# One Trainium2 core, a long convolution followed by a maxout FFN: the two sums over k1 of a tile placed step by step, and the first loop's stores, turns and drain rearranged

## The chip, the cores and the metric

The kernel runs on one core of a Trainium2 chip. The metric is device time in microseconds (us), the median of several executions. The profile is one execution, recorded instruction by instruction.

## The reference

Two layers follow each other. The first is a convolution as long as the sequence, computed with FFTs, whose filter comes from a small MLP; its output is multiplied by `x`. The second is a feed-forward layer that takes the maximum of three projections.

```python
# x, v: (4, 12544, 128); pos_emb: (12544, 64)
h_filt = (np.maximum(pos_emb @ w1, 0.0) @ w2) * np.exp(-0.01 * np.arange(S))[:, None]
u = x * v
Uf = np.fft.rfft(u, n=2 * S, axis=1)
Hf = np.fft.rfft(h_filt, n=2 * S, axis=0)
y = np.fft.irfft(Uf * Hf[None, :, :], n=2 * S, axis=1)[:, :S, :]
x = (x * y).reshape(B * S, 128)
h = np.maximum(np.maximum(x @ moe_w1, x @ moe_w2), x @ moe_w3)    # (50176, 768)
out = h @ moe_w_out                                               # (50176, 128)
```

All of it is float32.

## The kernel before, in words

TensorE (PE) does the transforms as matrix products in two stages, one over blocks of the sequence (index `k1`, 90 values, taken as 45 pairs `g`) and one inside a block. Besides PE there are VectorE (DVE), ScalarE (ACT), GpSimd (POOL) and the queue engine SyncE (SP). Every engine works through its own instructions in the order in which the Python code issues them[...]. A tile of a pool with `bufs=n` can be given out again only when the readers of the n-th tile before it are done, DMAs included. [...] a product that needs a bank waits until the engine that copies the former one out is done.

**Before the first loop** the filter and the first batch are brought into the first stage's spectrum.

**The first loop** (lines 991 to 1025) has one step `s` per pair `g`, 45 and a few to run out. PE does in a step, in this order: `s_second(s)` (`gps`, filter), `g_second(s)` (`ps`, signal), `s_filter(s-1)` (`sps`, two banks, one such tile), `g_third(s-3)` (`ps` again, from the pool `cps` of three banks that `g_second` uses too). Around them:

- `s_minus` (L931): POOL makes `minus`, the negated part of `specH`, for the next step's `gps`; one buffer.
- ACT copies `G` out of `gps`, `eo` out of `ps`, makes the two halves of `xs` (L547, L548), copies `ht` out of `sps` (L966) and `zs` out of the third product (L577).
- `ht` (two buffers) is multiplied in by DVE in `g_re` and `g_im`, and stored to `hd` in DRAM by two DMAs that POOL issues (L969), directly behind the copy. Later batches read `hd`.
- `zs` (two buffers) is stored to `zd` in DRAM by a DMA that ACT issues (L578).
- DVE does `g_re`, `g_im`, `g_unfold` (`ab`, which the third product reads) of pair `s-2`, and `g_butterfly` (`xt`) of pair `s`.
- SP loads the weights `wt` of both products three steps ahead (`load_dir`, L843), two loads of 256 KB a step.
- In the last 16 steps the first six units `u` of the second batch are loaded (`u_load`, L358), multiplied (`u_mul`, L365) and turned (`u_turn`: four PE transposes into a bank `pst` of `cps`, then an ACT copy). The turns come in pairs, 0 and 1 in step 36, 2 and 3 in step 41.

**The drain** (lines 988 to 1030) finishes the last pairs, and puts in between what the FFN needs: the product `lin` of `w1` and `w_out`, in six folds (`fold`: a transpose into `pt`, an ACT copy `w1t`, two products into the bank `pl`), and the first stage of six units (`unit`, two `u_first` each: PE products into a bank, ACT copy `high`, two DVE operations into `spec`).

**The FFN** has 32 tiles for each of the four batches. A tile has six steps `f`. In a step, `up` makes two products into the `hps` banks (three, in turn): ACT takes the first through Relu (L710), DVE takes the maximum with the second (L713, `hid`), and `down` of two steps before accumulates into `ops`. While the tiles of batch `b` go through, the convolution of batch `b+1` is spread over the 192 steps by `conv_steps`, a planner that holds an estimated DVE load of each step: `u_...` first, then pairs, each with two `g_quarter` products, `g_fold` (DVE takes the sum and the difference from PSUM, L496, after an ACT copy `eo`), `q_swap`, `q_re`, `q_im` and two `q_unfold`. Functions planned for a step run at its end.

The next tile's input is made beside: `t_load` fetches `zt`, `t_sums` makes the two sums over `k1` (`even` and, in place, `zt`; L678, L679, in half of the tiles L682 on DVE), and `t_last` does the last product and multiplies with `x` into `gt` (L700). Where no pairs are planned the sums run on POOL, else on DVE. Both come at once, in step 0 ahead of `up`:

```python
            if f == (3 if turn_ else 0):
                t_sums(tiles[n + 1], nc.vector if turn_ or i * NF > pairs_from else nc.gpsimd)
```

The planner allows for them with a fixed load in step 0 and for `t_last` with one in step 3:

```python
        load = [(1.2 if i % NF == 3 else 0.6) + (1.4 if i % NF == 0 and i > s0 else 0)
                for i in range(NT * NF)]
```

The last batch has no convolution beside it and another scheme of products; the change doesn't touch it.

Of the kernel before, what the change touches and what calls it, by code (L numbers as in the profile page):

```python
# [10 lines left out]
FP32 = mybir.dt.float32  # L11
# [5 lines left out]
P = 128  # L17
# [8 lines left out]
N1 = 90  # L26
# [65 lines left out]
def kernel(  # L92
# [279 lines left out]
    def u_turn(u):  # L372
        if u % 2 == 0:
            uts[u] = uts[u + 1] = utp.tile([NB, 16, 2, 32], FP32, tag="uT", name="uT")
        ps = state["turn"].tile([P, 512], FP32, tag="cv", name="pst")
        turn(u, ps)
        nc.scalar.copy(uts[u][:, 8 * (u % 2):8 * (u % 2) + 8],
                       ps[0:NB, :].rearrange("n (s t r) -> n s r t", s=8, r=2))
# [190 lines left out]
    def g_third(g):  # L569
        w, ab = ws.pop((g, 1)), abs_.pop(g)  # L570
        ps = state["cv"][1].tile([P, 512], FP32, tag="cv", name="ps3")
        for k in range(2):
            for q in range(2):
                halves_mm(ps[:, (2 * k + q) * D:(2 * k + q + 1) * D], w[:, k, q, :],
                          ab[:, k, q, :], k == 0 and q == 0, True)
        zs = state["cv"][0].tile([P, 2, 256], FP32, tag="z", name="zs", bufs=2)
        nc.scalar.copy(zs[:].rearrange("p k f -> p (k f)"), ps[:])  # L577
        nc.scalar.dma_start(  # L578
            zd[0][2 * g:2 * g + 2].rearrange("k c t f -> (c t) k f"), zs[:])

    def conv_steps(b, done):


        out = []

        def at(slot, late, fn, *args):
            out.append((slot, late, len(out), fn, args))

        per_pair = 170 / (NK + LATE + 0.6 * (NU - done))
        for u in range(done, NU):
            s = (u - done) * 0.6 * per_pair + 9
            at(max(0, int(s) - 9), 0, u_load, b, u)
            at(int(s) - 6, 0, u_mul, u)
            at(int(s) - 5, 0, u_planes, u)
            at(int(s) - 4, 0, u_dma, u)
            at(int(s), 0, u_join, u)
            at(int(s + 1), 1, u_first, u)
        s0 = int((NU - done - 1) * 0.6 * per_pair + 9) + 6  # L600

        def start(x):
            return s0 + int(x // 2 * 2 * per_pair)

        load = [(1.2 if i % NF == 3 else 0.6) + (1.4 if i % NF == 0 and i > s0 else 0)
                for i in range(NT * NF)]
        for x in range(NK + LATE):
            s = start(x)
            load[s] -= 1.2
            load[s + 1 + x % 2] += 1.4  # L610

        def emptiest(among, cost):
            s = min(among, key=lambda i: load[i])
            load[s] += cost
            return s

        for x in range(NK + LATE):
            s, odd = start(x), x % 2
            g, z = x if x < NK else None, x - LATE if x >= LATE else None
            at(s, 1, g_quarter, g, z)  # L620
            at(s + 1 + odd, 0, g_fold, g, z)
            at(s - 4, 0, w_load, x)
            if z is not None:
                at(s + 3 + odd, 0, g_store, b, z)
            if g is None:
                continue
            if g % 2 == 0:
                at(s - 4, 0, q_load, g, min(2, NK - g))
                at(s - 1, 0, h_load, g, min(2, NK - g))
            first = s + 2 + 2 * odd  # L630
            at(first, 0, q_swap, g, 0)
            at(first + 1, 0, q_swap, g, 64)
            last = start(x + LATE) - 1
            a = emptiest(range(first + 1, min(first + 3, last - 1) + 1), 0.7)
            at(a, 0, q_re, g)
            a = emptiest(range(a, min(first + 4, last - 1) + 1), 0.7)
            at(a, 0, q_im, g)
            for q in range(2):
                at(emptiest(range(a + 1, last + 1), 0.55), 0, q_unfold, g, q)
        slots = {}  # L640
        for s, _, _, fn, args in sorted(out, key=lambda r: r[:3]):
            slots.setdefault(s, []).append((fn, args))
        return slots, {start(x) + 1 for x in range(NK + LATE)}, s0


    N = 4 * NB
# [24 lines left out]
                              x[:, 4 * i:4 * i + 8, c, b, :])  # L671
        xTs[b, i], xTs[b, i + 1] = xT[:, 0], xT[:, 1]

    def t_sums(i, eng=nc.gpsimd):
        z0, z1 = zts[i]
        even = hp.tile([N1, 512], FP32, tag="even", name="even", bufs=2)
        if i[0] == 0 or i[1] < NT // 2:
            eng.tensor_tensor(out=even[:], in0=z0, in1=z1, op=ALU.add)  # L678
            eng.tensor_tensor(out=z1, in0=z0, in1=z1, op=ALU.subtract)  # L679
        else:  # L680
            for out, op in ((even[:], ALU.add), (z1, ALU.subtract)):
                nc.vector.scalar_tensor_tensor(out=out, in0=z1, scalar=sign_t[:, 0:1], in1=z0,  # L682
                                               op0=ALU.mult, op1=op)
        zts[i] = even[:], z1

    def t_last(i):
        zt = zts.pop(i)
# [218 lines left out]
    for i in (1, 2):  # L906
# [6 lines left out]
    cps = pro.enter_context(tc.tile_pool(name="cps0", bufs=3, space=PSUM))  # L913
    gps = pro.enter_context(tc.tile_pool(name="gps", bufs=2, space=PSUM))
    sps = pro.enter_context(tc.tile_pool(name="sps", bufs=1, space=PSUM))
    state = {"cv": (cvp, cps), "turn": cps, "xb": 2,
             "bank": lambda: cps.tile([P, 512], FP32, tag="cv", name="ps1")}
    pl = sps.tile([D, 512], FP32, name="pl")
    Gs, minus = {}, {}

    def fold(f):
        pt = cps.tile([P, 512], FP32, tag="cv", name="pt")
        nc.tensor.transpose(pt[:, 0:D], w_sb[0][:, f * P:(f + 1) * P], eye[:])
        w1t = cvp.tile([P, 2, D], FP32, tag="eo", name="w1t", bufs=2)
        nc.scalar.copy(w1t[:, 0], pt[:, 0:D])
        return lambda: halves_mm(pl[:, 0:D], w1t[:, 0], wo_sb[:, f, :], f == 0, f == NF - 1)

# [23 lines left out]
    def s_filter(g):  # L951
# [4 lines left out]
        for ri in range(2):  # L956
            for k in range(2):
                for q in range(2):
                    for h in range(2):
# [5 lines left out]
        ht = cvp.tile([P, 2, 2, 2, D], FP32, tag="ht", name="ht", bufs=2)  # L965
        nc.scalar.copy(ht[:].rearrange("p r k q d -> p (r k) q d"),  # L966
                       ps[:].rearrange("p (q m d) -> p m q d", q=2, d=D))
        for c in range(2):
            nc.gpsimd.dma_start(hd[g, 64 * c:64 * c + 64],  # L969
                                ht[64 * c:64 * c + 64, c].rearrange("p k q d -> p (k q d)"))  # L970
        hts[g] = ht

    EARLY = 6
    loads = dict(zip((NK - 16, NK - 14, NK - 12, NK - 9, NK - 8, NK - 4), range(EARLY)))
    muls = dict(zip((NK - 13, NK - 11, NK - 10, NK - 5, NK - 3, NK - 1), range(EARLY)))
    turns = {NK - 9: 0, NK - 4: 2}
    folded = []

    def folding(f):
# [4 lines left out]
    def unit(u):  # L984
        for h in range(2):
            u_first(u, 2 * h, 2)

    drain = {NK: [lambda: folding(0), lambda: folding(1), lambda: folded.pop()()],
             NK + 1: [lambda: folding(2), lambda: folding(3), lambda: folded.pop()(),
                      lambda: unit(0), lambda: unit(1)]}  # L990
    s_minus(0)
    for s in range(NK + 3):
        if s < NK:
            ws[s, 0] = wf[s]
            s_second(s)
            if s + 1 < NK:
                s_minus(s + 1)
            g_second(s)
            wf.pop(s)
            if s + 3 < NK:  # L1000
                wf[s + 3] = load_dir(s + 3, 0)
        if 1 <= s <= NK:
            g_swap(s - 1)
            s_filter(s - 1)
        if s >= 3:
            ws[s - 3, 1] = wi.pop(s - 3)
            g_third(s - 3)
            if s < NK:
                wi[s] = load_dir(s, 1)
        if 2 <= s <= NK + 1:  # L1010
            g_re(s - 2)
            g_im(s - 2)
            g_unfold(s - 2)
        if s < NK:
            g_butterfly(s)

        if s in muls:
            u_mul(muls[s])
        if s in turns:
            u_turn(turns[s])  # L1020
            u_turn(turns[s] + 1)
        if s in loads:
            u_load(1, loads[s])
        for job in drain.get(s, ()):
            job()
    u_turn(4)
    u_turn(5)
    folding(4)
    folding(5)
    folded.pop()()  # L1030
    nc.scalar.copy(lin[:], pl[:, 0:D])
    for u in range(2, 6):
        unit(u)
    pro.close()


# [22 lines left out]
    late = []  # L1059
    for n, (b, i) in enumerate(tiles[:LAST]):  # L1060
        if i == 0:
            beside, folds, pairs_from = conv_steps(b + 1, EARLY if b == 0 else 0)
        if n == 0:
            t_load(*tiles[0])
            t_load(*tiles[1])
# [2 lines left out]
        for f in range(NF):  # L1068
# [4 lines left out]
            elif i == NT - 1 and f < 2 and n + 1 + f < len(tiles):  # L1073
                t_load(*tiles[n + 1 + f])
            turn_ = i == NT - 1
            if f == 0:
                when = 4 if turn_ else min((3, 4, 2), key=lambda k: i * NF + k in folds)
            if f == (3 if turn_ else 0):
                t_sums(tiles[n + 1], nc.vector if turn_ or i * NF > pairs_from else nc.gpsimd)
            if f == 4 and n + 1 == LAST:  # L1080
                t_sums(tiles[n + 2], nc.vector)
            h = up((b, i), f)
            late.append(((b, i), f, h))
            if len(late) > 2:
                down(*late.pop(0))
            if f == when:
                t_last(tiles[n + 1])
            if f == 5 and n + 1 == LAST:
                t_last(tiles[n + 2])
# [100 lines left out]
```

## Time and profile before

| | |
|---|---|
| time, median of 3 runs | 2310.24 us (2307.21 to 2312.99) |
| profiled execution | 2310.21 us, span of the core 2308.4 us, PE clock 0.997 |
| up to the first loop | 0 to 117.8 us |
| first loop | 117.8 to 298.3 us |
| drain and first tile's input | 298.3 to 323.9 us, PE busy 17.57 of 25.60 us |
| FFN with convolution beside it, three batches | 323.9 to about 1890 us |
| last batch | about 1890 to 2308.4 us |
| DMA, whole run | 411.02 MB, mean 178 GB/s |
| DMA, 200 to 250 us (first loop) | 280 GB/s, mean busy share of the 16 engines 0.94 |

In the lines of the profile, `gps<-wt,minus` means that the instruction writes `gps` and reads `wt` and `minus`. Lines of the timeline have the start and the duration in us, the engine, the line of the code, the operation, the tiles, the shapes and how many were merged; in brackets stands the time for which the engine had been idle before, and who released it. "ACTq" and "SPq" are an engine's queue side, which issues DMAs. PEld is PE's load of weights. The page's shares are averages over stages with different limits.

### The profile page before, as it was taken

What the parts mean: (1) busy time and instruction counts of PE and PEld (TensorE: products, weight loads), DVE (VectorE), ACT (ScalarE), POOL (GpSimd) and SP (SyncE); (2) the same over time, 40 slices, a digit from 0 to 9 for tenths busy, and PEclk for the clock granted to TensorE, in tenths of its full rate; (3) what the DMA queues carried; (4) which work ended last, traced back from release to release, by engine and by line L of the source; (5) the groups of instructions that cost most, each with busy time, mean ns of one, the idle gap of its engine ahead of it and who ended that gap; (6) DMA issues with size and microseconds to landing.
All of it is one profiled execution on the core that took longest, in us unless ns stands there. A gap on an engine that the chain in (4) does not pass through costs nothing.

```text
span 2308.4 us, 68374 instructions
## 1 busy us (share of the span) xinstructions
PE 2270.3 (98%) x27855; PEld 1369.0 (59%) x27855; DVE 1575.3 (68%) x2856; ACT 1179.9 (51%) x2128; POOL 899.7 (39%) x1095
## 2 busy tenths in 40 slices
PE   8999989999999999999999999999999999999998
PEld 7989866655555546655555446655555446666665
DVE  5578856767887847758887847658888854445443
ACT  2678844456666534446666624446666632222222
POOL 2045424423333324423333324423333326666666
PEclk9999999999999999999999999999999999999999
DMA  7778969989998759969999849969999932222221
GB/s 176 191 216 266 289 164 190 157 188 241 234 239 221 197 125 192 187 145 240 247 245 247 211 118 194 186 146 244 246 248 240 221 93 55 55 59 68 65 55 22
DMA packets 473164, 411.02 MB, mean 178 GB/s; under 512 B 328005, under 2 KB 374232, under 8 KB 472850
## 3 DMA queue, kind: packets, MB, share of 16 engines
q1 hardware_dynamic: 433714, 317.68, 62.7%
q0 software_dynamic: 26416, 75.80, 11.3%
q10 hardware_dynamic: 12720, 13.18, 1.8%
q8 instruction: 219, 3.59, 0.7%
q14 instruction: 95, 0.78, 0.1%
HBM read 262.84 MB, written 84.67 MB: 151 GB/s over the span
## 4 chain that ended last, share of the span: by engine, by line
PE 83%; DMA 7%; ACT 3%; DVE 3%; issue 2%; SPq 1%; ACTq 0%; POOL 0%; DVEq 0%; POOLq 0%
PE hps L156 40%; PE ops L156 17%; PE ops L773 6%; PE cps L417 5%; PE cps L156 4%; PE ps L165 3%; PE cps L471 3%; PE cps L481 2%; DMA wt<-wq_const 2%; DMA ht<-hd 2%; DMA hd<-ht 2%; PE last L156 1%; ACT ht L966 1%; PE pst L370 1%; DMA zt<-zd 1%
## 5 line engine op out<-in xcount | busy, mean ns | idle before, releaser
L156 PE MATMUL hps<-gt,w_sb 128*64 128x392 f32 x6144 | 1149.6, 495 | 5.8 <-DVE hid L713 5.0
L710 ACT ACTIVATE hid<-hps 128x392 f32<-128x392 f32 x768 | 384.3, 500 | 734.7 <-PE hps L156 718.8
L156 PEld LDWEIGHTS hps<-gt,w_sb 128*64 128x64 f32 x6144 | 422.4, 137 | 438.7 <-issue 390.1
L713 DVE TENSOR_TENSOR hid<-hid,hps 128x392 f32<-128x392 f32 x768 | 427.8, 557 | 334.0 <-PE hps L156 329.6
L156 PE MATMUL ops<-hid,wo_sb 128*64 128x392 f32 x2304 | 477.9, 492 | 0.0
L523 POOL TENSOR_TENSOR cb<-cb,xs 128x512 f32<-128x512 f32 x135 | 181.9, 1347 | 471.7 <-DVE xs L520 327.1
L156 PEld LDWEIGHTS ops<-hid,wo_sb 128*64 128x64 f32 x2304 | 167.7, 137 | 211.5 <-issue 211.5
L496 DVE TENSOR_TENSOR cb<-cps,eo 128x512 f32<-128x512 f32 (+1 forms) x288 | 175.2, 650 | 66.4 <-ACT eo L493 65.9
L428 DVE TENSOR_TENSOR spec<-cps,high 128x360 f32<-128x360 f32 x180 | 135.2, 792 | 122.8 <-ACT high L426 122.8
L728 POOL DMA_DIRECT2D out_dram<-ot x96 | 75.1, 783 | 353.5 <-ACT ot L726 311.5
L511 ACT ACTIVATE xs<-cb 32x512 f32<-32x512 f32 x270 | 170.0, 630 | 22.6 <-DVE cb L496 13.9
L512 ACT COPY xs<-cb 32x512 f32<-32x512 f32 x270 | 166.7, 617 | 3.2
L426 ACT COPY high<-cps 128x360 f32<-128x360 f32 x90 | 71.9, 799 | 152.4 <-PE cps L417 125.7
L527 DVE TENSOR_TENSOR xs<-cb 128x256 f32<-128x256 f32 x270 | 142.0, 569 | 7.5 <-POOL cb L523 7.5
L417 PEld LDWEIGHTS cps<-f1q,uT 98*64 98x64 f32 x2880 | 124.1, 137 | 31.3 <-issue 30.6
L417 PE MATMUL cps<-f1q,uT 98*64 98x90 f32 x2880 | 127.7, 241 | 0.4 <-DVE uT L401 0.4
L386 POOL COPY planes<-ut 128x784 uint16<-128x784 uint16 x90 | 75.8, 842 | 113.0 <-DVE ut L365 110.2
L504 POOL DMA_DIRECT2D zd<-cb x135 | 92.9, 690 | 61.5 <-DVE cb L496 53.5
L156 PEld LDWEIGHTS cps<-f4p,even 90*64 90x64 f32 x1568 | 88.8, 138 | 37.6 <-issue 34.8
L515 DVE TENSOR_TENSOR cb<-cb,ht 128x512 f32<-128x512 f32 x135 | 92.3, 683 | 7.8 <-ACT xs L512 7.7
L156 PE MATMUL cps<-f4p,even 90*64 90x49 f32 x1568 | 95.7, 220 | 1.8 <-DVE even L678 1.8
L156 PE MATMUL cps<-f4p,zt 90*64 90x49 f32 x1568 | 97.0, 222 | 0.4 <-DVE zt L679 0.4
(137 smaller groups left out, 3195.7 us busy)
## 6 DMA issues: line engine op xcount, KB each, us to landing
ht<-hd SPq DMA_DIRECT2D x264, 256.0 KB, 6.8
wt<-wq_const SPq DMA_DIRECT2D x144, 256.0 KB, 6.8
zd<-cb POOLq DMA_DIRECT2D x135, 256.0 KB, 6.2
zt<-zd SPq DMA_DIRECT2D x384, 90.0 KB, 3.1
sq<-spec SPq DMA_DIRECT2D x264, 128.0 KB, 7.2
ut<-in_xr_dram SPq DMA_DIRECT2D x128, 196.0 KB, 4.3
ut<-in_vr_dram SPq DMA_DIRECT2D x128, 196.0 KB, 4.5
xT<-in_x_dram SPq DMA_DIRECT2D x256, 98.0 KB, 3.5
```

The source lines that it names most:

```text
L156: nc.tensor.matmul(out[64 * h:64 * h + 64], lhsT[:, 64 * h:64 * h + 64], rhs, start=start, stop=stop, skip_group_check=True)
L417: nc.tensor.matmul(ps[64 * c:64 * c + 64, 256 * i + h * N1:256 * i + (h + 1) * N1], t[:, 2 * ((at + i) % 8) + h].rearrange("n r t -> n (r ...
L428: nc.vector.tensor_tensor(out=spec[:, :, a, at:at + n], in0=v[:, 1], in1=high, op=op)
L496: nc.vector.tensor_tensor(out=cb[:, a, lo:hi], in0=ps[:, lo:hi], in1=eo[:, lo:hi], op=op)
L504: nc.gpsimd.dma_start(zd[b][2 * z:2 * z + 2].rearrange("k c t a f -> (k c t) a f"), zss.pop(z))
L511: nc.scalar.mul(xs[at:at + 32], xt[at + 32:at + 64], -1.0)
L512: nc.scalar.copy(xs[at + 32:at + 64], xt[at:at + 32])
L523: nc.gpsimd.tensor_tensor(out=xts[g], in0=xts[g], in1=xs[:], op=ALU.add)
L527: nc.vector.tensor_tensor(out=ab[:, q], in0=y[:, 0], in1=y[:, 1], op=(ALU.subtract, ALU.add)[q])
L710: nc.scalar.activation(h[:], pa[:, 0:N], Relu)
L713: nc.vector.tensor_tensor(out=h[:], in0=h[:], in1=pb[:, 0:N], op=ALU.max)
L773: nc.tensor.matmul(ps[64 * c:64 * c + 64, 0:H2], w, rhs[:, H2 * c:H2 * c + H2], start=start, stop=True, skip_group_check=True)
```

## The change

Five things, in two parts.

*First loop and drain.* (1) The store of `zs` is issued by SP instead of ACT. (2) The store of `ht` leaves `s_filter` and becomes `s_store`, called one step later, ahead of `g_re`; on POOL it then stands behind the next `minus` instead of in front of it. (3) The turns are spread, one each in steps 36, 37, 41 and 42, and use a bank of their own, the one that `pl` has later. (4) In the step after the last pair, both remaining pairs go through `s_store`, `g_re`, `g_im` and `g_unfold`; unit 0 comes there, the two remaining third products follow before any fold, and folds, units and turns alternate after them. `w1t` takes the buffers of `G`, and the units take their banks in turn from `gps` and `cps`, five instead of three.

*FFN.* (5) `t_sums` can make one of its two sums alone, and runs behind `up` instead of ahead of it. `conv_steps` picks for every tile the steps of the two sums (the emptiest of steps 0 and 1 for the first, the emptiest from there to the step before `t_last` for the second) and the step of `t_last`, before it places `q_re`, `q_im` and `q_unfold`. Where the sums run on POOL they stay in step 0; in the last tile of a batch they stay in step 3. The two `q_unfold` of a pair are put in order of their steps.

No operation is added or taken away: the same matmuls, DVE, ACT and POOL operations and DMAs are issued, 45 of the DMAs from another engine.

```diff
-        nc.scalar.dma_start(
+        nc.sync.dma_start(
             zd[0][2 * g:2 * g + 2].rearrange("k c t f -> (c t) k f"), zs[:])
...
-        load = [(1.2 if i % NF == 3 else 0.6) + (1.4 if i % NF == 0 and i > s0 else 0)
-                for i in range(NT * NF)]
+        load = [0.6] * (NT * NF)
...
+        plan = []
+        folds = {start(x) + 1 for x in range(NK + LATE)}
+        for i in range(NT - 1):
+            s = i * NF
+            last = min((3, 4, 2), key=lambda k: s + k in folds)
+            load[s + last] += 0.6
+            if s <= s0:
+                plan.append((0, 0, last))
+                continue
+            a = emptiest(range(s, s + 2), 0.7) - s
+            plan.append((a, emptiest(range(s + a, s + last), 0.7) - s, last))
+        plan.append((3, 3, 4))
...
+            two = sorted(emptiest(range(a + 1, last + 1), 0.55) for _ in range(2))
             for q in range(2):
-                at(emptiest(range(a + 1, last + 1), 0.55), 0, q_unfold, g, q)
+                at(two[q], 0, q_unfold, g, q)
...
-    state = {"cv": (cvp, cps), "turn": cps, "xb": 2,
-             "bank": lambda: cps.tile([P, 512], FP32, tag="cv", name="ps1")}
-    pl = sps.tile([D, 512], FP32, name="pl")
+    free = itertools.cycle([(gps, "g"), (cps, "cv")])
+
+    def bank():
+        pool, tag = next(free)
+        return pool.tile([P, 512], FP32, tag=tag, name="ps1")
+
+    state = {"cv": (cvp, cps), "xb": 2, "bank": bank,
+             "turn": lambda: sps.tile([P, 512], FP32, tag="pl", name="pst")}
...
-        w1t = cvp.tile([P, 2, D], FP32, tag="eo", name="w1t", bufs=2)
+        w1t = cvp.tile([P, 2, D], FP32, tag="G", name="w1t", bufs=2)
...
+        hts[g] = ht
+
+    def s_store(g):
         for c in range(2):
-            nc.gpsimd.dma_start(hd[g, 64 * c:64 * c + 64],
-                                ht[64 * c:64 * c + 64, c].rearrange("p k q d -> p (k q d)"))
-        hts[g] = ht
+            nc.gpsimd.dma_start(
+                hd[g, 64 * c:64 * c + 64],
+                hts[g][64 * c:64 * c + 64, c].rearrange("p k q d -> p (k q d)"))
...
-    turns = {NK - 9: 0, NK - 4: 2}
+    turns = {NK - 9: 0, NK - 8: 1, NK - 4: 2, NK - 3: 3}
...
-    drain = {NK: [lambda: folding(0), lambda: folding(1), lambda: folded.pop()()],
-             NK + 1: [lambda: folding(2), lambda: folding(3), lambda: folded.pop()(),
-                      lambda: unit(0), lambda: unit(1)]}
...
-        if 2 <= s <= NK + 1:
-            g_re(s - 2)
-            g_im(s - 2)
-            g_unfold(s - 2)
+        for g in {NK: (s - 2, s - 1)}.get(s, (s - 2,)):
+            if 0 <= g < NK and s <= NK:
+                s_store(g)
+                g_re(g)
+                g_im(g)
+                g_unfold(g)
...
-    u_turn(4)
-    u_turn(5)
-    folding(4)
-    folding(5)
+        if s == NK:
+            unit(0)
+    pl = sps.tile([P, 512], FP32, tag="pl", name="pl")
+    state["turn"] = bank
+    for f, then in enumerate(((unit, 1), (unit, 2), (u_turn, 4), (u_turn, 5), (unit, 3), None)):
+        folding(f)
+        if then:
+            then[0](then[1])
     folded.pop()()
     nc.scalar.copy(lin[:], pl[:, 0:D])
-    for u in range(2, 6):
-        unit(u)
+    unit(4)
+    unit(5)
...
-            if f == (3 if turn_ else 0):
-                t_sums(tiles[n + 1], nc.vector if turn_ or i * NF > pairs_from else nc.gpsimd)
...
             h = up((b, i), f)
+            for a in range(2):
+                if f == plan[i][a]:
+                    t_sums(tiles[n + 1],
+                           nc.vector if turn_ or i * NF > pairs_from else nc.gpsimd, (a,))
```

## The prediction

> **What bounds the kernel now.** I read the shares, then the chain of waits, then the longest idle stretches of TensorE (PE) one by one, and last the timeline around each.
>
> ```profile
> PE 2270.3 (98%) x27855; PEld 1369.0 (59%) x27855; DVE 1575.3 (68%) x2856; ACT 1179.9 (51%) x2128; POOL 899.7 (39%) x1095
> PE 83%; DMA 7%; ACT 3%; DVE 3%; issue 2%; SPq 1%; ACTq 0%; POOL 0%; DVEq 0%; POOLq 0%
> ```
>
> PE carries the whole; only its pauses and slow stretches can be won, so I price those. The change touches three places: the first loop (117.8 to 298.3 us), its drain (298.3 to the first FFN matmul at 323.94) and the FFN (to about 1890).
>
> In the loop a step's matmuls of PE last 0.87 (`gps`) + 0.87 (`spec`) + 1.03 (`sps`) + 1.02 (third) = 3.80 us, and from 131.39 to 150.42 five steps take 3.81 each. But the copies of `ht` start at 151.00 and, 25 steps on, at 250.27: 3.97 a step. The timeline of one step:
>
> ```profile
> 202.32 0.13 PEld L943 LDWEIGHTS gps<-wt,minus 128*64 128x64 f32 x1 [0.28 <-POOL minus L931]
> ...
> 203.62 0.59 ACT L577 COPY zs<-ps 128x512 f32<-128x512 f32 x1
> 204.03 1.11 POOL L969 DMA_DIRECT2D hd<-ht  x2 [1.76 <-ACT ht L966]
> 204.25 0.40 ACTq L578 DMA_DIRECT2D zd<-zs  x1
> 204.68 0.37 ACT L948 COPY G<-gps 128x256 f32<-128x256 f32 x1 [0.47 <-PE ps L156]
> 205.16 1.01 POOL L931 TENSOR_SCALAR minus<-specH 128x128 f32<-128x128 f32 x1
> ...
> 206.64 1.01 ACT L966 COPY ht<-sps 128x1024 f32<-128x1024 f32 x1
> 207.55 0.59 ACT L577 COPY zs<-ps 128x512 f32<-128x512 f32 x1
> ```
>
> ACT goes round from `zs` to `zs` in 3.93 us without a pause other than the 0.47 in which it issues its own store. POOL makes `minus` only after the store of `ht`, and PE waits 0.28 for it. So ACT and this POOL order hold the step above PE's 3.80.
>
> ```profile
> DMA to landing us min/median/max: 3.8/4.8/7.5
> ```
>
> These are the `hd` stores from 200 to 250 us. `ht` has two buffers: a copy waits until the store of two steps before has landed. Read one by one, that landing came within 0.15 us of the copy's start in 8 of 41 cases, usually about 1 us earlier.
>
> ```profile
> 264.95 0.62 PE L370 MATMUL pst<-eye,ut 128*98 128x128 f32 x4 [1.07 <-DVE xt L182]
> 303.69 0.66 PE L156 MATMUL pl<-wo_sb,w1t 128*64 128x128 f32 x8 [1.93 <-ACT w1t L925]
> 321.44 0.32 PE L156 MATMUL cps<-f4p,even 90*64 90x49 f32 x4 [1.83 <-DVE even L678]
> ```
>
> The first is the second turn of a pair waiting for a bank; the others are the largest of 8.0 us of PE pauses in the drain. In the FFN, PE pauses for 8.8 us in all, and this is most of it:
>
> ```profile
> PE hps L156 <- DVE hid L713: 5.0, 10, 0.6
> ```
>
> ```profile
> 573.99 1.29 DVE L496 TENSOR_TENSOR cb<-cps,eo 128x512 f32<-128x512 f32 x2 [1.22 <-ACT eo L493]
> 575.19 0.68 DVE L678 TENSOR_TENSOR even<-zt 90x512 f32<-90x512 f32 x1
> 575.90 0.69 DVE L679 TENSOR_TENSOR zt<-zt 90x512 f32<-90x512 f32 x1
> 576.51 0.55 DVE L713 TENSOR_TENSOR hid<-hid,hps 128x392 f32<-128x392 f32 x1
> 577.12 1.54 PE L156 MATMUL hps<-gt,w_sb 128*64 128x392 f32 x8 [0.43 <-DVE hid L713]
> ```
>
> A fold (1.29) and both sums (1.37) stand in front of a maximum on DVE, and PE lacks its bank. All ten pauses (0.42 to 0.55 each) are of this form, at the start of tiles 14, 15, 22, 23 of the first batch and 15, 20, 26 of the next two.
>
> **What the Trainium skill says.** "DMA: Bandwidth & Descriptors", section "Issuing engines are not separate DMA queues": another issuing engine saves only the sequencer's issue time. The trace agrees on that price: 0.40 of ACT per store. The same page, "Queues, rings and completion order": SP and ACT each own a row of rings, and a DMA engine takes turns between the rows with work. A `zd` store moved to SP then lines up with the weight loads, while `hd`, on POOL's, has one row fewer to share with; no trace here shows either. "SBUF — State Buffer", section "Who interferes with whom": a DVE operation with two SBUF inputs and a GpSimd operation that reads SBUF shut each other out. The trace agrees: `minus` takes 0.58 or 1.01 us.
>
> **The change part by part**, against the span of 2308.4.
>
> 1. *`zd` store from ACT to SP.* 45 x 0.40 us leave ACT; its round becomes 3.5, and DVE's, from 295.34 to 299.00 without a wait, is 3.66. PE's 3.80 is then the longest. On SP the store waits for `zs`, and the second weight load of the step is queued behind it. In the trace third ends at 206.3 and `zs` at 208.2, so that load goes 2.3 us later with the issue; it is used three steps on, about 8 us after, against a median landing of 4.5: hidden. Where an upload of `ut` stands behind it too, another store's issue is added, hidden by the same slack. Unknown is the landing of `zd` itself: 5.0 median now. `zs` has two buffers, so two steps must hold 0.59 + 0.2 + landing; at 3.80 it may take 6.8. I take 5.5; bounds 4.5 and 8.
> 2. *`ht` store behind `minus`.* The 0.28 for `minus` goes, as does one pause of 0.89 at 127.54 behind the first store. In return the store is queued behind `minus`, which starts once `gps` has been read (0.95 into the step) and ends by 2.0. `ht` ends at 0.8, so the store goes up to 1.0 later against its copy. Copy 1.0, wait 1.3, second issue 0.57, landing 4.8 make 7.7 against two steps of 7.6; but `ht` can be late by some 0.8 before PE's next `sps` lacks its bank. So a stall needs a landing over 5.6, as about 10 of 43 had, mostly by 0.3. I take 0.06 a step.
>    Loop from 151 to 250: 25 x (3.97 - 3.86) = 2.8; bounds 25 x 0.17 = 4.1, and 0 (below nothing: the last rival). With the 0.9 of the start, 3.7.
> 3. *Turns one to a step, in `pl`'s bank.* From 249.81 to 298.34 eleven steps took 48.5, against 11 x 3.80 + 4 turns x 0.64 = 44.4. Of the 4.2 over, 1.07 + 0.85 are second turns waiting for a bank; they go. 1.05 is a late `hd` landing, the rest slow steps. I take 2.5, bounds 0.5 and 4.2. The turn's copy (0.53 on ACT) now falls on four steps instead of two.
> 4. *Drain.* Same matmuls, other order: both last thirds before the folds, units between folds, five banks instead of three. Pauses now 8.0 in 25.6. Left are the last `ab` of DVE (PE waits about 1.7 for it, with unit 0 ahead), some 0.4 at `sps`, 0.5 among units, and the tail from unit 5 over sums, `last` and `gt`, which stays at 1.83 + 0.40 + 0.76 = 3.0. 8.0 - 5.6 = 2.4; I take 2.0, bounds 0.5 and 3.5. The last `zd` store is issued about 4 us earlier, but `zt` was already there when DVE came to it, so that earns nothing.
> 5. *Sums placed apart, FFN.* No operation is added. In the changed program's order of DVE the sums come behind a maximum instead of ahead of it, and no fold stands in front of both any more: what lies between two maxima with a sum there was up to 3.9 us (24 times a fold and both sums, 2.7, ten of them with a pause), and is now at most 2.8. Whoever waits for the sums, `last` two or three steps on, still has a step. At the ten places this takes out 0.7 or 1.4 us ahead of a maximum that was 0.42 to 0.55 late. I take 4.7 of 5.0; bounds 2.5 and 5.5. The sums on POOL before the pairs only change places with PE's issue: nothing, POOL being idle for over half.
>
> Sum: 3.7 + 2.5 + 2.0 + 4.7 = 12.9, a span of 2295.5. The profiled execution took 2310.21, the median of the three runs is 2310.24 (2307.21 to 2312.99), so I take 12.9 from that: 2297.3.
>
> **Rivals.**
> - *The `hd` landing replaces ACT as the loop's bound.* For it: 8 of 41 copies waited already. Against: one row fewer beside it. The steps stay at 3.97; left are 0.9 + 1.9 + 2.0 + 4.7 = 9.5: 2300.7.
> - *The moved sums bring their pause with them, so the FFN part doesn't do what it says.* For it: 23 places now have both sums, a `re` and an `im` behind one maximum, 2.7 us. Against: blocks of 3.9 without a fold waiting for ACT made no pause before. Gain 12.9 - 4.7 = 8.2: 2302.0. With the first rival 4.8: 2305.4.
> - *Slower: the `zd` store waits in SP's row.* For it: in the FFN, SP's `wt` and `ht` loads land in 6.8. Against: the loop's own land in 4.5. `zs` then waits for its buffer and ACT stands still. It holds the step above today's 3.97 from a landing of 7.1 on; at 8 a step is 4.4, 41 x 0.43 = 17.6 lost, less 1 + 2 + 4.7 won: 2320.
>
> **How the numbers follow.** 0.3%, 6.9 us, is about what a measurement of this kernel can tell from no change: the line is at 2303.3. My forecast 0.56 (2292 to 2302.5), first rival 0.17, second 0.10, both 0.08, slower 0.09. Faster: 0.56 + 0.15 + 0.06 = 0.77; same: 0.02 + 0.04 + 0.08 = 0.14; slower 0.09. With all best bounds the gain is 18.2, so the range begins at 2292 and reaches over the joint rival to 2307; the slower case and a little at the ends are left out.
>
> **What would show it.** Right: `ht` copies 3.80 to 3.88 apart, no wait of `gps` for `minus`; `zd` landing under 6.5; no second turn waiting for `xt`; first FFN matmul about 8 us earlier; `hps` waiting for `hid` under 1 us in all. Wrong: ACT `zs` or `ht` waiting for a DMA in most steps, PE waiting for `wt` in the loop, or ten pauses of `hps` at other steps.

## The result, and the profile after

| | before | after |
|---|---|---|
| median of six runs each | 2309.92 us (2307.21 to 2312.99) | 2303.24 us (2298.90 to 2306.36) |
| ratio, 95% interval | | 0.9968 (0.9953 to 0.9983) |
| profiled execution, its span | 2310.21, 2308.4 us | 2306.36, 2304.6 us |
| loop: first `gps` to `gps` of step 44 | 176.58 us | 171.62 us |
| drain: from there to the first `hps` | 29.57 us | 32.23 us |
| FFN: from there to the first product (`last`) made for the last batch's other scheme | 1569.80 us | 1569.47 us |
| rest | 414.66 us | 414.67 us |

By the medians the kernel is 6.7 us faster, where 12.9 were forecast; by the ratio of the runs it is 0.32%, with an interval from 0.17 to 0.47%. The loop gave about what it should, the drain took some back and the FFN gave nothing. The profiled execution is the slowest of the six, and we will see why. These four rows are of one execution each. The start of the loop isn't in the table: it lies between 116.2 and 120.0 us in the executions below, in a part that nobody changed.

The first line of the page after:

```profile
PE 2266.4 (98%) x27855; PEld 1373.2 (60%) x27855; DVE 1559.5 (68%) x2856; ACT 1175.1 (51%) x2128; POOL 874.7 (38%) x1095
```

The engines have as many instructions as before, and PE is still busy almost throughout. Such a line can't tell what happened, so on to the three parts.

**Loop.** Timeline of one step after the change (ACT, POOL and SP's queue):

```profile
160.14 0.59 ACT L577 COPY zs<-ps 128x512 f32<-128x512 f32 x1
160.32 0.52 POOL L955 TENSOR_SCALAR minus<-specH 128x128 f32<-128x128 f32 x1 [2.04 <-PE gps L967]
...
160.76 0.37 SPq L578 DMA_DIRECT2D zd<-zs  x1
160.80 1.10 POOL L996 DMA_DIRECT2D hd<-ht  x2
163.01 1.01 ACT L990 COPY ht<-sps 128x1024 f32<-128x1024 f32 x1
...
163.92 0.59 ACT L577 COPY zs<-ps 128x512 f32<-128x512 f32 x1
```

From `zs` to `zs` it is 3.78 us, where it was 3.93. POOL makes `minus` as soon as `gps` has been read, and the store comes behind. At that place `minus` runs beside DVE operations that read PSUM (`eo,ps`) and takes 0.52 us in the median; before, it mostly ran beside sums of two SBUF tiles (`xt,xs`) and took 1.01. The undisturbed step is 3.80 to 3.81 us, PE's own sum. But not all steps are undisturbed. PE's waits in the loop after, and the largest of them in the timeline:

```profile
PE sps L985 <- ACT ht L990: 2.7, 3, 1.2
PE gps L967 <- DMA wt<-wt_const: 1.0, 1, 1.0
```

```profile
201.10 1.01 ACT L990 COPY ht<-sps 128x1024 f32<-128x1024 f32 x1 [2.16 <-PE ps L156]
...
202.17 1.10 PE L985 MATMUL sps<-w2x,G 64*64 64x128 f32 x31 [1.18 <-ACT ht L990]
```

The profile names PE's `ps` as what ACT waited for, but that was long done. The store of the same buffer, two steps before, was issued at 194.12 and landed at 201.02; the copy starts 0.08 us later. That is the `hd` landing of the first rival. The `hd` stores of 200 to 250 us landed in:

```profile
DMA to landing us min/median/max: 3.4/5.1/6.9
```

That is no sooner than before (median 4.8), although `zd` has left ACT's queue.

**Drain.** PE at the largest pause of the drain after, then stretches cut where the granted clock changes (length, busy time of PE, PEld, DVE, ACT and POOL, then PEclk, DMA share and GB/s):

```profile
300.02 1.30 PE L156 MATMUL ps<-ab,wt 128*64 128x128 f32 x16 [2.08 <-DVE ab L565]
...
301.65 2.67 PE L417 MATMUL ps<-f1q,uT 98*64 98x90 f32 x32
```

```profile
297.51:300.92 3.41, 1.33 (x24) 1.02 (x20) 3.27 (x8) 1.45 (x4) 1.05 (x2) 1.00 0.66 162
300.92:304.34 3.42, 3.42 (x40) 2.69 (x36) 0.95 (x4) 1.23 (x3) 0.00 (x0) 0.50 0.62 182
304.34:307.75 3.41, 3.41 (x38) 2.98 (x38) 1.19 (x4) 1.09 (x3) 0.00 (x0) 0.50 0.11 22
```

The pauses of the drain are shorter in sum than before (6.46 us against 8.03). But behind this one the granted clock is 0.50 for 6.8 us, and 32 matmuls of a unit take 2.67 us instead of 1.41. Before, the clock was 1.00 from 295 to 320 us. So PE is busy for 25.77 us of the drain after, where the same matmuls took 21.55 before. No list of waits shows this loss, since PE counts as busy; the column PEclk does.

**FFN.** PE's waits in the FFN after; the ten pauses of `hps` for `hid` (5.0 us) are gone from the list, and in their place stand:

```profile
PE cps L156 <- DVE zt L698: 4.0, 13, 0.6
PE cps L156 <- DVE zt L700: 3.3, 8, 0.6
```

One of these places in the timeline after:

```profile
546.24 1.26 POOL L523 TENSOR_TENSOR cb<-cb,xs 128x512 f32<-128x512 f32 x1 [1.08 <-DVE xs L520]
546.40 1.66 DVE L698 TENSOR_TENSOR zt<-zt 90x512 f32<-90x512 f32 x1
...
548.11 0.32 PE L156 MATMUL cps<-f4p,zt 90*64 90x49 f32 x4 [0.56 <-DVE zt L698]
```

`last` needs both sums. The planner put the second one into the step right before `last`, behind that step's maximum, and there it is late: by 0.15 to 0.22 us in 12 places, and by 0.54 to 0.62 in nine. In these nine the sum took 1.66 us instead of 0.68 (0.74 in the tiles with L700), and POOL was adding `cb` at the same time in every one of them.

### The profile page after: what moved, and what is told of

Same layout as the page of the kernel before. It is cut to its first block, busy times and chain, and to the rows that moved or that the text cites. A ratio compares the mean times of both kernels' runs of the same rounds, so it can differ in the third digit from the quotient of the medians.

```text
span 2304.6 us, 68557 instructions
## 1 busy us (share of the span) xinstructions
PE 2266.4 (98%) x27855; PEld 1373.2 (60%) x27855; DVE 1559.5 (68%) x2856; ACT 1175.1 (51%) x2128; POOL 874.7 (38%) x1095
## 4 chain that ended last, share of the span: by engine, by line
PE 85%; DMA 7%; DVE 4%; issue 1%; ACT 1%; SPq 1%; POOL 0%; DVEq 0%; ACTq 0%; POOLq 0%
PE hps L156 38%; PE ops L156 15%; PE ops L792 6%; PE cps L417 5%; PE cps L156 4%; PE ps L156 3%; PE ps L165 3%; PE cps L471 3%; DMA ht<-hd 3%; PE cps L481 2%; PE sps L985 2%; PE gps L967 1%; PE last L156 1%; DMA wt<-wq_const 1%; DMA zt<-zd 1%
## 5 line engine op out<-in xcount | busy, mean ns | idle before, releaser
L523 POOL TENSOR_TENSOR cb<-cb,xs 128x512 f32<-128x512 f32 x135 | 175.7, 1301 | 479.6 <-DVE xs L520 389.8
L527 DVE TENSOR_TENSOR xs<-cb 128x256 f32<-128x256 f32 x270 | 146.8, 588 | 3.9 <-POOL cb L523 3.9
L816 POOL DMA_DIRECT2D out_dram<-o x128 | 77.4, 610 | 49.7 <-DVE o L809 47.8
```

The source lines that it names most:

```text
L523: nc.gpsimd.tensor_tensor(out=xts[g], in0=xts[g], in1=xs[:], op=ALU.add)
L527: nc.vector.tensor_tensor(out=ab[:, q], in0=y[:, 0], in1=y[:, 1], op=(ALU.subtract, ALU.add)[q])
```

## The experiments

All medians are of five runs or more, and each ratio is to runs of the kernel before on the same chip. Loop, drain and FFN are those of the one profiled execution, between the marks of the table above.

| kernel | median us (lowest to highest) | ratio to before (95%) | loop | drain | FFN |
|---|---|---|---|---|---|
| e1_loop_only | 2301.24 (2296.76 to 2307.93) | 0.9958 (0.9943 to 0.9973) | 167.47 | 27.69 | 1569.92 |
| e2_ffn_only | 2310.63 (2306.10 to 2314.18) | 0.9998 (0.9989 to 1.0006) | 175.98 | 29.56 | 1567.89 |
| e3_sums_early | 2299.91 (2298.27 to 2302.20) | 0.9951 (0.9939 to 0.9963) | 169.14 | 29.66 | 1566.19 |
| e4_ht3 | 2313.83 (2308.49 to 2322.62) | 1.0013 (1.0004 to 1.0022) | 176.34 | 32.37 | 1570.99 |
| e5_drain_fill | 2300.35 (2299.15 to 2301.22) | 0.9955 (0.9942 to 0.9967) | 168.77 | 27.33 | 1568.88 |
| e6_zd_act | 2303.58 (2300.94 to 2308.84) | 0.9966 (0.9952 to 0.9979) | 171.37 | 33.24 | 1569.15 |
| e7_store_first | 2303.91 (2300.08 to 2305.01) | 0.9967 (0.9954 to 0.9979) | 169.84 | 30.92 | 1571.30 |
| e8_sums_room | 2300.72 (2299.11 to 2301.93) | 0.9955 (0.9943 to 0.9968) | 169.91 | 29.61 | 1566.26 |
| e9_again (the changed kernel) | 2302.72 (2299.48 to 2303.86) | 0.9959 (0.9947 to 0.9971) | 169.26 | 29.42 | 1570.18 |
| e10_fill_early | 2297.98 (2297.49 to 2301.07) | 0.9947 (0.9934 to 0.9960) | 167.42 | 27.08 | 1567.09 |
| e11_short_prefetch | 2317.20 (2311.57 to 2318.76) | 1.0023 (1.0014 to 1.0032) | 177.21 | 37.17 | 1571.46 |
| e12_one_sum | 2298.49 (2290.85 to 2302.36) | 0.9938 (0.9923 to 0.9954) | 168.49 | 32.65 | 1562.31 |

### Each half alone: e1_loop_only and e2_ffn_only

The first has edits 1 to 4, with `conv_steps`, `t_sums` and the FFN's loop as before; the second has edit 5 alone.

> The changed first loop and drain with the FFN part as before. Theory (the FFN part exchanges one wait for another and earns nothing): the whole gain of the change is here, 5 to 8 us under before; in the trace the ten pauses of hps for hid (5.0 us) are there and no pause of cps for zt. Rival (the FFN part earns its 4.7 as forecast, the loop little): 1 to 3 us under before.

> The first loop and drain as before, with the FFN part of the change alone. Theory: within 1.5 us of before; hps no longer waits for hid, and PE pauses about 7 us in some 21 places where cps waits for the second sum (zt), nine of them with a zt operation of 1.66 us. Rival (forecast): 4 to 5 us under before.

The half with the loop and the drain alone has the whole gain; the FFN's half alone has a ratio of 0.9998, with an interval (0.9989 to 1.0006) that holds 1. So what the change gains, it gains ahead of the FFN.

### The second sum a step earlier: e3_sums_early

```diff
-            plan.append((a, emptiest(range(s + a, s + last), 0.7) - s, last))
+            plan.append((a, emptiest(range(s + a, s + last - 1), 0.7) - s, last))
```

> The changed kernel, but the second sum may not be placed in the step right before the last product. Theory (the new wait comes from that step): the pauses of cps for zt fall from 7.3 us to under 1.5, hps for hid stays under 1, so 5 to 7 us under the changed kernel, about 2297. Rival (DVE has no room for both sums in steps 0 and 1): pauses of hps for hid come back, 3 us or more, and the time is that of the changed kernel within 2 us.

The waits for `zt` fall from 7.3 to 0.3 us, no wait for `hid` returns, and the FFN takes 3.3 us less than after, below the 1567.9 to 1571.3 of all executions with the change's FFN. But a third wait has come, in eight places:

```profile
PE cps L471 <- DVE gt L719: 6.9, 8, 0.9
```

In those tiles `last` shares its step with quarter products, and the second of these needs the bank that `gt` empties. `gt` is late on DVE. How long single tiles take in the first batch, counted from ACT's `hid` of one tile to that of the next:

| tile | before | after | sums early |
|---|---|---|---|
| 11 (pause for `zt` of 0.15 to 0.22 after) | 15.50 | 15.86 | 15.50 |
| 13 (pause for `zt` of 0.56 after) | 16.17 | 16.78 | 16.94 |
| 14 (pause for `hid` before) | 16.13 | 15.48 | 15.50 |
| 15 (pause for `hid` before) | 15.75 | 15.11 | 15.09 |

Over the three batches, and without two tiles that changed for other reasons, 16 tiles became 0.29 to 0.77 us shorter, 8.9 in sum, and 21 became 0.30 to 0.68 longer, 9.8 in sum. (The two are the first tile, 0.83 longer because the clock behind the drain was low for longer, and one whose wait of 1.15 for weights was gone, 1.39 shorter.) So the FFN's half did what it was said to do, and more, and lost it again in as many places. A short pause costs more than its figure: 0.15 to 0.22 in the list is 0.30 to 0.36 in the tile.

### A third buffer for `ht`: e4_ht3, and its control e11_short_prefetch

A third `ht` doesn't fit beside three buffers of weights, so e4 has three of `ht` and two of weights, loaded two steps ahead; e11 has only the second half of that.

```diff
-    lwp = pro.enter_context(tc.tile_pool(name="lwp", bufs=3))
+    lwp = pro.enter_context(tc.tile_pool(name="lwp", bufs=2))
...
-        ht = cvp.tile([P, 2, 2, 2, D], FP32, tag="ht", name="ht", bufs=2)
+        ht = cvp.tile([P, 2, 2, 2, D], FP32, tag="ht", name="ht", bufs=3)
...
-            if s + 3 < NK:
-                wf[s + 3] = load_dir(s + 3, 0)
+            if s + 2 < NK:
+                wf[s + 2] = load_dir(s + 2, 0)
...
```

> The changed kernel with three buffers for ht instead of two; to make room, the weights of the first loop have two buffers instead of three and are loaded two steps ahead. Theory (landings of hd stores cause the loop's pauses of sps for ht and the late last ht in the drain): those pauses (3.5 us in the loop, 0.8 and part of 2.1 in the drain) go, steps are 3.80 to 3.82, 3 to 6 us under the changed kernel. Rival (they come from the DMA traffic, and whoever is next waits for it): PE waits for wt instead, and the time is that of the changed kernel or above.

> The changed kernel with only the control's half of the run with three ht buffers: loop weights in two buffers, loaded two steps ahead; ht stays at two buffers. Theory: with weights only two steps ahead (7.6 us less 2.3 of waiting behind the zd store) the loads land too late, PE waits for wt as in the run with three ht buffers, and waits of sps for ht are still there too; loop 175 to 180, median 2312 or above. Rival: in that run the third ht buffer itself did harm (more stores in flight, slower landings); then the loop here is 170 to 173, median 2303.

PE's waits for weights in the loop, of e4 and then of e11:

```profile
PE gps L967 <- DMA wt<-wt_const: 6.5, 7, 2.2
```

```profile
PE gps L967 <- DMA wt<-wt_const: 5.6, 6, 1.6
```

Both loops are as slow as before the change (176.34 and 177.21), so the loss is the shorter prefetch's. Whether it needs the store that now waits in SP's queue ahead of a load was not tested. Neither list has a wait for `ht`, so these two runs don't tell what the third buffer does; what it would bring with three buffers of weights was not measured.

### Undoing the loop's edits one at a time: e6_zd_act and e7_store_first

```diff
-        nc.sync.dma_start(
+        nc.scalar.dma_start(
             zd[0][2 * g:2 * g + 2].rearrange("k c t f -> (c t) k f"), zs[:])
```

> The changed kernel with the zd store issued by ACT again; everything else as changed. Theory (step 1 of the forecast): ACT's round is 0.40 longer again and the steady step goes from 3.81 back to 3.90 to 3.95, the loop (first gps to gps of step 44) from 171.6 to 175 or 177; median 2306 to 2308. Rival: the order of store and minus on POOL was what held the step, and the step stays at 3.81 to 3.84, loop under 173; median 2303.

```diff
         hts[g] = ht
+        s_store(g)
...
-                s_store(g)
                 g_re(g)
```

> The changed kernel with the hd store issued right behind the copy of ht again, ahead of minus in POOL's order; zd stays on SP. Theory (step 2 of the forecast): gps waits for minus again, about 0.28 us in many steps, the step goes to 3.9 or above and the loop to 174 or more; median 2305 or above. Rival: with ACT no longer late, ht ends 0.8 us into a step, store and minus are done 2.9 us into it, and nobody waits for minus; the store then goes up to 1 us earlier, the stalls of sps for ht (0.83, 0.73, 1.18 and 1.00 in the changed kernel's profile) go, and the loop takes 167.5 to 169; median 2300.

With the store on ACT, ACT has this in every step (timeline of e6):

```profile
163.78 0.59 ACT L577 COPY zs<-ps 128x512 f32<-128x512 f32 x1
164.80 0.37 ACT L972 COPY G<-gps 128x256 f32<-128x256 f32 x1 [0.44 <-ACT zs L577]
...
167.66 0.59 ACT L577 COPY zs<-ps 128x512 f32<-128x512 f32 x1
```

The round is 3.88 us here and the step 3.89: ACT's queue was the bound, as forecast. Its loop, 171.37, lies inside the spread of the kernels with both edits (167.4 to 171.6), and its median inside the range of the changed kernel's runs, so what this edit alone is worth in time is not shown. (Some 28 steps of 0.08 come to 2.2 us; against the mean of those loops, 169.0, it is 2.4.) With the store's order undone and `zd` on SP, the undisturbed step stays at 3.81, no steady step waits for `minus`, and PE's list has no wait for `ht`; only the pause of 0.89 behind the first store comes back, which makes its step 1.3 longer. The forecast's step 2 had the order as a gain in each step. It is a small one as long as ACT is late (3.94 a step before, 3.89 in e6); once `zd` is on SP, the order is worth the start and, as far as this one execution shows, no more.

### The pause in the drain: e5_drain_fill and e9_again

```diff
-        if s == NK:
-            unit(0)
+        if s in (NK, NK + 1):
+            unit(s - NK)
...
-    for f, then in enumerate(((unit, 1), (unit, 2), (u_turn, 4), (u_turn, 5), (unit, 3), None)):
+    for f, then in enumerate(((unit, 2), (u_turn, 4), (u_turn, 5), (unit, 3), None, None)):
```

> The changed kernel with unit 1 moved ahead of the folds, to stand between the last two third stages (unit 0 there already); nothing else. Theory: the 2.08 us pause of TensorE before the last third stage (waiting for DVE's last ab) is what opens the pauses of 292 to 300 us, and these let the granted clock fall to 0.59 and 0.72 in the two slices after. With 2 us of matmuls put in, the pause shrinks to under 0.6, the clock stays at 0.95 or more from 300 to 310 us, and the drain (gps of step 44 to first hps) takes 26 to 28.5 us instead of 32.2; median about 2300, ratio to the kernel before 0.995 to 0.996. Rival: the clock falls from pauses elsewhere or by chance of the execution; the drain then stays over 30 us with slices under 0.75, and the median at 2303.

> The changed kernel once more, beside the others of this call on one chip. Theory: what differs between executions of it is where hd landings stall sps in the loop and how far the clock falls in the drain, so its median stays at 2302 to 2304, and its profile shows a loop of 168 to 172, a drain of 29 to 33 with a clock below 0.85 in the slices right behind the 2 us pause at about 300 us, and an FFN part of 1569 to 1570. Rival: the drain of 32.2 us was one odd execution; then drain under 28.5 and clock at 1.00 there, median at 2300 as with unit 1 moved.

With unit 1 between the last two third products the pause ahead of the last one is 0.84 us, the clock stays at 1.00 until 310 us, and the drain takes 27.33. The changed kernel, run again, has the pause of 2.09 us (297.10 to 299.19) but not the clock's fall behind it:

```profile
294.94:298.35 3.41, 2.08 (x42) 1.69 (x38) 2.54 (x5) 2.64 (x5) 1.04 (x2) 1.00 0.73 213
298.35:301.77 3.42, 2.58 (x49) 2.23 (x49) 1.98 (x7) 1.05 (x3) 0.00 (x0) 1.00 0.73 199
```

So the same pause has two outcomes. Of seven executions with a pause of 2.05 to 2.10 us there (after, e1, e3, e7, e8, e9, e12), three show the fall, for 6.8, 3.4 and 10.2 us (after, e7, e12), with drains of 32.23, 30.92 and 32.65; four don't, with 27.69 to 29.66. In the two executions with the short pause (e5, e10) there is none, with 27.33 and 27.08. The fall isn't bound to that pause either: e6, with pauses of 1.51 and 1.61, has one of 10.2 us and a drain of 33.24, and the longest drain, 37.17 in e11, has one of 13.7 us behind a wait of 2.19 for weights.

The Trainium skill, "TensorE: Matmul & The Clock Gate", section "What's actually happening", says that the clock follows an activity window of some 3.4 us that runs freely, so that its phase against the program differs from run to run. The traces show it. In each of the fourteen profiles the clock changes only at times that are whole multiples of 3.41 us apart. Cut at these times, the changed kernel's pause lay within one window in the first profile, which left PE busy for 1.33 of 3.41 us there (under "Drain" above), and was split between two in e9 (2.08 and 2.58). Counted from 120 us on over all fourteen profiles, the clock fell behind each of the 18 windows at full clock in which PE was idle for 1.8 us or more, behind two of the five with 1.6 to 1.8, and behind none of the some 8800 with less. Once fallen, it stayed at 0.50 for one to four windows, though PE was busy throughout most of them; what sets that length stays open.

The section "HAM oscillation — how this bites in real kernels" states the rule as no idle gap over about 3.4 us. Here no single gap in the drain is over 2.2, and the clock falls all the same: what counted was the idle time in one window, about half of it. For this kernel the rule is not strict enough.

Behind the tail of the drain (the sums, `last` and `gt`) the clock falls in every profile, before too, and is at 0.50 into the FFN. The tail differs in one more way. In e3, e7, e8 and e9 the first tile's second sum on DVE took long (1.70 us in e9), since POOL made one of the next tile's sums just then; PE waited 1.30 to 1.45 instead of 0.35. In e9 that sum of POOL was released by the landing of `zt`, so which of the two comes first depends on when `zt` lands.

### Room ahead of `last`: e8_sums_room, and one sum less: e12_one_sum

e8 is e3 and a reserve in the plan:

```diff
             load[s + last] += 0.6
+            load[s + last - 1] += 1.2
```

> The changed kernel with the second sum at the latest two steps ahead of last (as in the run sums early) and 1.2 us reserved for the planner in the step ahead of last, so that no four unfolds stand there. Leaves the rest. Theory: what is left in sums early is the wait of the quarter products for the bank that gt empties behind four unfolds (6.9 us); with at most three unfolds there these waits fall under 2.5 us, the waits for the sums stay at 0.3 or less, hps for hid at 1 or less; FFN part 1564 to 1565 us against 1569.5 changed and 1566.2 in sums early; median 2298 to 2299. Rival: what is taken from one step comes back in the next as pauses of hps for hid (3.3 us of DVE between two maxima in the step before); FFN part 1566 or above, median 2300 or above.

The rival is nearer, for another reason than it gave: in the places I read the unfolds ahead of `gt` went from four to three, the wait for `gt` stayed at 6.7 us in eight places, and the FFN at 1566.26. My reason, four unfolds in one step, fell. The busy time of DVE in the stretch around such a place (after, 1158.8 to 1168.0 us; columns PE, PEld, DVE, ACT, POOL) suggests another:

```profile
1158.80:1168.00 9.20, 8.58 (x132) 5.13 (x130) 9.17 (x16) 5.60 (x10) 3.39 (x4) 1.00 1.00 251
```

DVE is busy for 9.17 of 9.20 us: over these four steps it is the bound, and order inside them only decides who waits. (0.92 us of it is the second sum's wait beside POOL; in e3, where no operation is drawn out at this place, DVE is busy for 9.25 of 9.30 us.) e12 is e3 with work taken away. In the stage of the pairs it leaves out the second sum, and `last` takes the odd half as it was loaded, so the result lacks this part:

```diff
-            if a not in parts:
+            if a not in parts or left_out:
...
+                           a == 1 and not turn_ and i * NF > pairs_from)
```

> The run sums early with the second sum of each tile left out where it would lie on DVE in the stage of the pairs (the odd half then goes into last as it was loaded, so this part of the computation is missing); the first sum stays. Theory: where last shares its step with quarter products, DVE has work without a gap from a fold to the next re and im (9 us in the changed kernel from 1158.8 to 1168.0), and a pause of TensorE can only move inside it; with 0.75 us less in it the wait for gt's bank falls from 6.9 us in all to under 2.5, FFN part 1562 to 1564.5 us (1566.2 in sums early). Rival: the wait comes from the chain of fold, store and add on ACT and POOL, not from DVE's amount of work; then it stays at 5 us or more and the FFN part at 1565.5 or above.

```profile
PE cps L471 <- DVE gt L719: 3.0, 8, 0.4
```

With 0.75 us less DVE work the eight waits fall by 0.49 each, from 6.9 to 3.0 us, and the FFN to 1562.31, 3.9 less than in e3. The wait came down a little less than expected (under 2.5). But it followed the amount of DVE's work, with the chain over ACT and POOL as it was, so that amount is the cause of more than half of it; the rest was not taken apart.

### Both additions: e10_fill_early

> The changed kernel with both additions that gained: unit 1 between the last two third stages, and the second sum at the latest two steps ahead of last. Theory: the two act in different parts and add up: drain 26.5 to 28.5, FFN part 1565.5 to 1567, loop as it falls at 167 to 171; median 2297 to 2298.5, ratio to the kernel before 0.9940 to 0.9948, better than both kernels. Rival: what they win is the spread of the executions and not the parts; median 2300 as for either alone.

2297.98 us, by the medians faster than both kernels (clear of the kernel before; the runs of the changed kernel, 2299.48 to 2303.86 beside it, overlap its upper end): the drain and the FFN each keep what they won (27.08 and 1567.09), and this execution had no stall in the loop (167.42). The two additions act in different parts and add up.

## Why the prediction was right or wrong

The sign was right, and the time lies in the range. The size isn't that of the likeliest case (12.9 us) but near the second rival's (8.2): 6.7. That it fell in the range is partly luck: two of the four terms that made up the 12.9 came to nothing or less, and the other two, of the loop, gave more than forecast. By its steps:

- *Step 1, `zd` to SP: right.* ACT's round bound the steady step; e6 puts it back and has 3.89 instead of 3.81. `zd` landed in 4.6 us median (5.5 taken) and no step waited for it; the slower rival didn't come. The weight loads, partly put later behind the store, were not fully hidden: they landed in 5.5 us median instead of 4.4, with one wait of 1.00 in the profile after and one of 0.46 in e9.
- *Step 2, the store's order: half right.* The landing of `hd` is a bound in single steps, as the working had it. But that the order gains in the steady step failed: e7 undoes it and has the same 3.81. What it wins is the first pause. The order may also delay a store: e7's list has no wait of PE for `ht`, after has three; but e1 and e10, with the new order, have none either.
- *Steps 1 to 3, the loop in all: right in mechanism, a little small in size.* The forecast was 0.9 + 2.8 + 2.5 = 6.2. In the eight executions with both edits (after, e1, e3, e5, e8, e9, e10, e12) the loop took 167.4 to 171.6, 169.0 in the mean: 7.6 less than the 176.6 before, 7.0 less than e2's 176.0. The spread comes mostly from the stalls for `hd` and `wt`: e1 and e10, which have none, took 167.5 and 167.4. No second turn waits for a bank any more.
- *Step 4, the drain: wrong.* The sum counted pauses only. They did get 2.1 us shorter in e1 (5.9 us of PE pauses against 8.0), and its drain is 1.9 shorter, as taken. But over the six executions of this drain with the loop as changed (after, e1, e3, e8, e9, e12) the mean is 30.2, 0.6 longer than before: the pauses are 1.4 shorter (6.6), and PE's busy time is 2.1 longer (23.6 against 21.55), of which an estimated 1.9 is the clock (half of the busy time at 0.50). The term that failed is "Left are the last `ab` of DVE (PE waits about 1.7 for it ...)": it was 2.1, and it was taken to cost its own length, when it can cost the clock too. A second one is the tail that "stays at 1.83 + 0.40 + 0.76 = 3.0": in e3, e8 and e9 it was 4.0 to 4.1.
- *Step 5, the FFN: wrong.* The pauses of `hid` went, all ten. The sentence that failed is "Whoever waits for the sums, `last` two or three steps on, still has a step". The planner's range ends at the step before `last`, and the 21 second sums behind the new waits had no step to spare. It cost 9.8 us in those tiles, against 8.9 won. The rival had the size right for another reason: not a late maximum moved, but a new wait of `last`. And behind it stands what the forecast didn't ask: whether DVE has any idle time in those steps. In the stretch that was read it has 0.03 us in 9.2.

The ledger: 7.6 from the loop, less 0.6 in the drain, FFN nothing (1569.8 in the mean of after and e9, against 1569.8; the low clock at its start is in it, about 1.4 us before and 2.2 and 2.5 in these two) gives 7.0; measured are 6.7 and, with the changed kernel run again as e9 (2302.72 against 2311.53), 8.8.

## What to carry to other kernels

Before moving an operation to an emptier step, look up who reads it and where that reader stands, and leave a whole step between; then ask of the stretch as a whole, not of the step, whether its engine has idle time. If it has none, the pause moves and doesn't go. In an order written by hand, add up TensorE's pauses over any 3.4 us, not one by one: here 1.8 us of them in one window always cost the clock, and under 1.6 never did. Put independent matmuls in between, and read the clock behind the pauses as well as the list of waits. One profile isn't enough for such a place, since the same pause can lie differently in the windows each time.

## What the hardware showed

A DVE sum with two SBUF inputs (90x512) took 1.66 us instead of 0.68 where POOL's add of 1.26 us ran at the same time. The Trainium skill, "SBUF — State Buffer", section "Who interferes with whom", says that the two shut each other out; this is the price here, and nine of the 21 new waits are of that form.

TensorE's clock fell to half behind windows of 3.41 us with 1.8 us or more of idle time, and stayed there for one to four windows. Behind the pause before the last third product PE was busy all through the fall, so its three falls of 6.8, 3.4 and 10.2 us (after, e7, e12) cost an estimated 3.4, 1.7 and 5.1 us, half of their length each; the pause itself was 2.1.
